# Sliding attention and a state-space convolution in one kernel: u kept in SBUF, v stored with its halo, the last matrix loaded by blocks, transfers split over two queues

## The chip, the cores and the metric

The kernel runs on one core of a Trainium2 chip. The core has five engines that run their own instruction streams: TensorE (PE; its weight loads are listed apart as PEld), VectorE (DVE), ScalarE (ACT), GpSimd (POOL) and SyncE (SP). SP, POOL and ACT also issue DMA transfers. The metric is the time of one launch in device microseconds; lower is better.

## The reference

Two independent computations over S = L = 2048 rows and D = 640 columns, put side by side in the output.

```python
# A: sliding, dilated attention. 32 heads of 20, window 8, dilation 2
q, k, v = x @ wqkv, split into heads
idx = pos[:, None] - (arange(8) * 2)[None, :]          # a row sees itself and 7 rows before it, 2 apart
logits = einsum("hsd,hswd->hsw", q, k[:, idx]) * 20 ** -0.5, -1e9 where idx < 0
a = einsum("hsw,hswd->hsd", softmax(logits), v[:, idx]).merge_heads() @ wo
# B: S4 convolution, 192 complex states for each of 640 channels
K[d, l] = real(sum_n C[d, n] * exp(dt[d] * A[d, n] * l) * dt[d] * B[d, n])
b = irfft(rfft(pad(u)) * rfft(pad(K)))[:, :2048] + u * Dskip
return concatenate([a, b], axis=-1)                    # 2048 x 1280
```

## The kernel before

**Part A (class `PartA`).** The rows go in four blocks of 512. `proj` multiplies x by wqkv for 128 columns at a time (L747), ScalarE copies the result to a staging tile `st` (L750), and SP stores it in DRAM: v to `vd` (L753), q and k to `qkd` (L755). Both have 14 columns of zeros in front (`halo`, L732 to L737, by POOL), so that a window that reaches back 14 rows always finds data. For block b, `fetch` (L767) reads five tiles `qk` of 128 channels back, each with 14 rows more, into three buffers; `fetch_v` (L780) reads v as 20 d's by 128 partitions (two halves of 256 rows, two parities of the window, 32 heads) into one tile of 8 d's and one of 12, with four transfers for each. `logits` multiplies q by shifted k on VectorE (`prod`, L793, ten for a block), sums over a head's channels on TensorE (L800) and makes the softmax; `av` multiplies attn by v (`p`, L842, ten for a block), sums on TensorE (L850); `out_proj` (L867 to L872) applies wo.

**Part B.** The channels go in five chunks c of 128, held as 4 groups of 32 (partitions: state or time index, depending on the stage). `Prep` makes tables of powers of exp(dt A); `Tables` builds for each chunk an x table (`Xtab`, with the gathered powers `Xg`, L539) and a y table (`Ytab`, L543; `ypos`, then `yneg`, L562 and L563, which multiplies by `mag`, L557). `kgen` (L596, L603) forms the convolution kernel from them on TensorE, ScalarE copies it (`Kd`, L617), SP moves Kd within SBUF (L584), and `spread` (L637, L642) lays it out as K. `f1` (L658) and `f2` (L678, `Sp` L683) transform K and the input u, whose chunk SP loads as tile `U` by four transfers of 64-byte runs (L1059). `swap` (L1073) brings the halves of a spectrum to the other partitions by two transfers; `product` (L688, L689) multiplies spectra on VectorE; `ia` (L703, L706) does the first inverse stage, whose Z is stored in DRAM for chunks 0 to 2 (L1084). At the end `inverse` adds, for each of 64 positions l, the identity times uD (u times Dskip, L1131) and the last inverse matrix HB times z (L1134), copies (L1137) and stores (L1139). HB is 128 x 128 for each l and each of real and imaginary part, zero outside four diagonal blocks of 32 x 32; eight transfers of 512 KB load it whole (L1103), eight of 320 KB load uD (L1108).

**The order.** Each function hands its work out as named pieces for the engines P, V, A, G (POOL and its queue) and S (SP's queue). `TRACE`, a recorded text, gives the order in which the pieces are created; `SEQ` gives each engine's own order, one engine after another; `SLOTS` says which buffer of a ring each piece takes. Every engine runs its list in that order. `attention_pool`, `fft_pool` and `inv_pool` free the SBUF of one phase for the next: HB and uD take the place of the tables (`tab`) and can be loaded only when the last `kgen` is done with them. In part A's names, `fetchv3.S` is a piece of `fetch_v(3)` on SP; in part B's, `yneg4` is `yneg` of chunk 4.

Of the kernel before, what the change touches and what calls it, by code (L numbers as in the profile page):

```python
# [18 lines left out]
CW = 192  # L19
# [6 lines left out]
S = 2048; D = 640; H = 32; DH = 20; W = 8; DIL = 2; HALO = 14; PB = 512; PH = 256  # L26
# [101 lines left out]
def att_consts_np():  # L128
    gs = np.zeros((128, 5, 32)); hs = np.zeros((128, 32)); sm = np.zeros((128, 128)); sw = np.zeros((128, 128)); mk = np.zeros((128, 4, 16))
    for p in range(128):  # L130
        for ct in range(5):
            gs[p, ct, (128 * ct + p) // DH] = 1.0
        hs[p, p % 32] = 1.0
        sm[p, 64 * (p // 64) + p % 32] = sm[p, 64 * (p // 64) + 32 + p % 32] = 1.0
        sw[p, p ^ 32] = -1.0
    for w in range(1, W):
        mk[32 * (w // 4):32 * (w // 4) + 32, 3 - w % 4, 0:DIL * w] = -1e9
    return dict(Gs=gs.reshape(128, 160), Hs=hs, Sm=sm, Sw=sw, Mk=mk.reshape(128, 64))
# [7 lines left out]
load.G weights.P mag0.A x1.S weights.A prep.V load.G weights.P weights.A gens0.V load.G prep.V weights.P weights.A gens0.V x1.S load.G prep.V
weights.V weights.A weights.P am0.A load.G prep.V am0.A weights.V am0.A wq.S load.G am0.A:2 x1.S set.G weights.V am0.A set.G am0.A:2 weights.V
am0.A:2 load.G x1.S weights.V am0.A prep.A weights.V load.G k0.P weights.S gens1.V load.G x2.S gens1.V load.G gens0.A gens1.A load.G gens1.V gens0.A
k0.P load.G gens1.A gens1.V load.G x3.S gens1.A weights.V gens1.A gens1.V k0.P genm0.V k0.A gens1.V x1.S gens1.A q0.P weights.V k0.A wv.S gens1.A
gens1.V q0.P weights.V x2.S q0.A gens1.V q0.P gens1.A x2.S weights.V k0.A q0.P weights.V gens1.A gens0.V x2.S weights.V q0.A q0.P gens0.V gens0.A  # L150
gens0.V gens0.A gens0.V q0.A weights.S k0.P gens0.V genm0.V gens0.A x2.S gens0.V gens0.A gens0.V gens0.A k0.P genm0.V gens0.A gens0.V gens0.A
gens0.V gens0.A x3.S genm0.V k0.A gens0.V:2 k0.A genm0.V gens0.V gens0.A xtab0.V k0.S v0.P gens0.A v0.P gens0.A gens0.V x3.S xtab0.V gens0.A xtab0.V
q0.A gens0.V:2 v0.P q0.A genm0.V gens0.V gens0.A xtab0.V q0.S gens0.A:2 gens0.V k1.P x3.S xtab0.V gens0.A gens0.V gens0.A gens0.V gens0.A xtab0.V
gens0.V gens0.A k1.P genm0.V gens0.A x3.S genm0.V xtab0.V k1.P xtab0.V genm0.V v0.A xtab0.V k1.P v0.A xtab0.V genm0.V v0.A xtab0.V k1.P v0.P genm0.V
xtab0.V am1.A xtab0.V v0.P v0.A genm1.V am1.A xtab0.V genm1.S v0.A k1.A v0.S q1.P:2 k1.A genm1.V k1.A q1.P k1.A gens1.V k1.A xtab0.V q1.P am1.A k1.S
xtab0.V genm1.S am1.A xtab0.V q1.P am1.A genm1.V v1.P am1.A xtab0.V genm1.S q1.A v1.P q1.A gens1.V q1.A v1.P xtab0.V q1.A genm1.V q1.A v1.P am1.A
q1.S xtab0.V genm1.S am1.A gens1.V k2.P xtab0.V am1.A k2.P xtab0.V am1.A v1.A gens1.V k2.P am1.A xtab0.V v1.A k2.P xtab0.V v1.A ypos0.V v1.A k2.P
ypos0.V k2.A ypos0.V:2 k2.A v1.P k2.A:2 ypos0.V k2.A ypos0.V v1.A k2.S q2.P yneg0.V q2.P v1.S q2.P gens1.A ypos0.V gens1.A q2.P gens1.A gens1.V q2.P
genm1.V q2.A:2 gens1.V v2.P genm1.S q2.A:2 ypos0.V q2.A v2.P gens1.A q2.S v2.P gens1.A gens1.V genm1.V gens1.A v2.P gens1.V v2.A genm1.S v2.A v2.P
genm1.V gens1.A k3.P gens1.V v2.A genm1.S ypos0.V v2.A:2 k3.P gens1.V gens1.A v2.S q3.P gens1.V gens1.A genm1.V gens1.A q3.P gens1.V genm1.S gens1.A  # L160
q3.P genm1.V gens1.A k3.A gens1.V genm1.S q3.P q3.A genm1.V q3.A q3.P gens1.V q3.A genm1.S q3.A ypos0.V k3.P q3.A gens1.A q3.S yneg0.V v3.P gens1.A
v3.P k3.A genm1.V k3.A v3.P yneg0.V genm1.S attpool fetch0.S v3.P gens1.A mag1.A fetch0.S v3.A:2 v3.P v3.A mag1.A:2 kgen03.P tab1.S mag1.A:2 wo.S
mag1.A:2 fetch0.S mag1.A k3.P mag1.A logits0.V fetchv0.S mag1.A:2 fetchv0.S mag1.A k3.P mag1.A fetchv0.S logits0.V mag1.A:3 k3.A kgen03.P logits0.V
fetch0.S k3.A v3.A k3.S logits0.P v3.A kgen02.P xtab1.V kgen03.A v3.S fftpool logits0.V fetchv0.S xtab1.V:2 logits0.V xtab1.V:5 logits0.P xtab1.V
kgen00.P xtab1.V:2 kgen00.P logits0.V xtab1.V:2 logits0.V u0.S fetch0.S xtab1.V u0.S logits0.P kgen00.A kgen01.P xtab1.V:2 u0.S xtab1.V kgen01.P
xtab1.V logits0.V u0.S xtab1.V:2 logits0.V logits0.P fetch1.S kgen01.A kgen02.P xtab1.V:2 kgen02.A ypos1.G taby1.S logits0.V ypos1.G taby1.S:2
xtab1.V logits0.P taby1.S xtab1.V taby1.S logits1.V T.S u0.P logits0.A u0.P kd0.S u0.A u0.P ypos1.V kd0.S u0.P u0.A logits1.V fetch1.S u0.P u0.A
u0.P fetchv0.S u0.P u0.A kd0.S ypos1.V u0.P ypos1.V u0.A logits0.V kd0.S u0.A u1.S ypos1.V u0.A:2 logits0.V ypos1.V logits0.P ypos1.V logits0.V
ypos1.V logits0.P spec.P logits0.A spec.P:2 spec.A fetchv0.S spec.A ypos1.V spec.P spec.A:2 spec.P spec.A tab2.S spec.A spec.P spec.A wo.S spec.A
logits1.V spread0.P fetch1.S spread0.P spec.A spread0.P spread0.A spread0.P fetch1.S spread0.A ypos1.V u1.S spread0.A ypos1.V spec.A:3 logits0.P  # L170
yneg1.V spread0.A spec.P:2 spec.A spread0.P spec.A spread0.P:2 spread0.A spread0.P yneg1.V spread0.P spec.A spread0.P spec.A spread0.P logits0.A
spread0.P mag2.A logits0.P mag2.A xtab2.V mag2.A u1.S logits0.A yneg1.V logits0.A mag2.A xtab2.V mag2.A kgen13.P xtab2.V mag2.A logits0.V mag2.A:3
wo.S mag2.A kgen13.P xtab2.V mag2.A swap0.S mag2.A:2 xtab2.V fetchv0.S xtab2.V mag2.A xtab2.V mag2.A u1.S spread0.A xtab2.V spread0.A xtab2.V
# [1016 lines left out]
```

## Time and profile before

| | before |
|---|---|
| time, median of 3 runs | 368.86 us (365.17 to 370.67) |
| the profiled execution: time, span | 369.83 us, 368.0 us |
| granted TensorE clock, mean | 0.903 |
| DVE busy | 305.1 us, 83% |
| PE busy | 292.8 us, 80% |
| ACT busy | 257.2 us, 70% |
| DMA | 119,210 packets, 65.49 MB, 178 GB/s over the span; 76,192 packets under 512 B |
| SP queue's share of 16 DMA engines | 71.6% |

The span is the time from the first to the last instruction of the profiled execution; the rest of its time, 1.8 us, lies outside. "Busy" counts an engine's instructions, not the issue of transfers. Ends of matmuls are modelled, so TensorE's busy time says less than the starts of its instructions do. In a line of groups the name before the arrow is what is written, the ones behind it are read; "idle before" is the time in which the engine stood idle just ahead of these instructions, with what ended the wait. "Issue" names idle time in which nothing that the profile shows was waited for.

### The profile page before, as it was taken

How to read it: one execution, taken by the hardware profiler on the slowest of the kernel's cores; microseconds unless marked ns; L12 is line 12 of the kernel's file. 1: busy time of each engine (PE TensorE's matmuls, PEld its weight loads, DVE VectorE, ACT ScalarE, POOL GpSimd, SP SyncE). 2: the span in 40 equal slices, each digit the busy share in tenths (PEclk: the TensorE clock that was granted, in tenths of full speed). 3: DMA queues.
4: the chain of work that ended last, by engine and by line, in shares of the span. 5: the costliest groups of instructions: out<-in, count | busy, mean ns of one | idle time of the engine just before them, and what ended most of it. 6: DMA issues, size and time to landing. Idle time of an engine off the chain costs nothing. (4 is left out here: it accounts for less than half of the span.)

```text
span 368.0 us, 13345 instructions
## 1 busy us (share of the span) xinstructions
PE 292.8 (80%) x5808; PEld 195.3 (53%) x5808; DVE 305.1 (83%) x397; ACT 257.2 (70%) x574; POOL 35.6 (10%) x72
## 2 busy tenths in 40 slices
PE   2959999999654486777989796888988748889984
PEld 1414444445431375555666564567855546557763
DVE  1896999795899988998999998799999935568940
ACT  2978899898600588357999645797779304779773
POOL 9740000000000000000000000000000000002750
PEclk9978999999665678899999899997999966999999
DMA  7999683697978987566976355860768756999885
GB/s 152 204 205 213 185 269 117 202 287 228 263 140 147 238 210 134 139 161 95 205 99 156 121 133 109 228 150 15 142 213 235 257 209 101 190 219 192 227 191 136
DMA packets 119210, 65.49 MB, mean 178 GB/s; under 512 B 76192, under 2 KB 115712, under 8 KB 118000
## 3 DMA queue, kind: packets, MB, share of 16 engines
q1 hardware_dynamic: 116320, 61.61, 71.6%
q0 software_dynamic: 1776, 2.79, 3.7%
q8 instruction: 45, 0.74, 0.9%
q10 hardware_dynamic: 1056, 0.25, 0.3%
q14 instruction: 13, 0.11, 0.1%
HBM read 35.25 MB, written 21.03 MB: 153 GB/s over the span
## 5 line engine op out<-in xcount | busy, mean ns | idle before, releaser
L747 PE MATMUL ps_p<-xT,w 128*128 128x512 bf16 x300 | 69.9, 397 | 4.1 <-DMA w<-in_A_wqkv_dram 4.1
L603 PE MATMUL ps_k<-Ytab,Xtab 64*20 64x33 bf16 (+1 forms) x2560 | 52.9, 247 | 11.7 <-issue 11.7
L842 DVE TENSOR_TENSOR p<-vb,attn 128x2048 bf16<-128x2048 bf16 x40 | 47.5, 1218 | 12.4 <-PE ps_o L850 10.3
L603 PEld LDWEIGHTS <-Xtab 64*20 64x20 bf16 (+1 forms) x2560 | 47.6, 123 | 17.0 <-issue 14.7
L793 DVE TENSOR_TENSOR prod<-qk 128x2048 bf16<-128x2048 bf16 x40 | 48.1, 1224 | 10.0 <-DMA qk<-qkd 7.5
L747 PEld LDWEIGHTS <-w 128*128 128x128 bf16 x300 | 30.2, 102 | 43.0 <-issue 6.2
L683 ACT CAST Sp<-ps_f 128x512 bf16<-128x512 f32 (+1 forms) x96 | 43.1, 613 | 7.0 <-PE ps_f L678 6.7
L662 ACT CAST A<-ps_f 128x512 bf16<-128x512 f32 x80 | 41.4, 619 | 7.1 <-PE ps_f L658 6.8
L617 ACT CAST Kd<-ps_k 128x264 bf16<-128x264 f32 x20 | 7.9, 394 | 47.0 <-PE ps_k L603 47.0
L750 ACT CAST st<-ps_p 128x512 bf16<-128x512 f32 x60 | 31.7, 609 | 7.1 <-DMA qkd<-st 3.1
L800 PE MATMUL ps_l<-prod,cGs 128*32 128x512 bf16 x160 | 21.5, 464 | 17.2 <-DVE prod L793 17.1
L678 PE MATMUL ps_f<-A,cT 64*128 64x128 bf16 (+1 forms) x768 | 27.7, 214 | 7.3 <-ACT Sp L683 3.5
L678 PEld LDWEIGHTS <-cT 64*128 64x128 bf16 x768 | 21.6, 98 | 16.4 <-issue 11.3
L706 ACT CAST Z<-ps_ia 128x512 bf16<-128x512 f32 x40 | 21.7, 632 | 5.6 <-PE ps_ia L703 5.6
L850 PE MATMUL ps_o<-p,cHs 64*32 64x256 bf16 x640 | 21.7, 288 | 4.1 <-DVE p L842 4.1
L867 PE MATMUL ps_op<-wo,oT 128*128 128x320 bf16 x160 | 24.4, 300 | 0.3 <-ACT oT L856 0.2
L547 POOL MEMSET Ytab<- 128x192 bf16 x5 | 1.3, 258 | 238.3 <-PE ps_k L603 134.4
L557 ACT ACTIVATE mag<-ta 128x192 bf16<-128x192 f32 x80 | 22.8, 404 | 0.0
L1139 POOL DMA_DIRECT2D out_dram<-ys x24 | 14.4, 608 | 76.8 <-ACT rc L826 70.2
L703 PE MATMUL ps_ia<-cE,Sp 128*128 128x128 bf16 x160 | 20.5, 224 | 0.7 <-DVE Sp L689 0.4
L510 DVE TENSOR_TENSOR krtmp<-Xtab,Xg 128x3072 bf16<-128x3072 bf16 (+1 forms) x15 | 20.3, 1356 | 0.1
L703 PE MATMUL ps_ia<-cE,UT 128*128 128x128 bf16 x160 | 20.4, 224 | 0.0
(113 smaller groups left out, 531.3 us busy)
## 6 DMA issues: line engine op xcount, KB each, us to landing
qk<-qkd SPq DMA_DIRECT2D x20, 263.0 KB
qkd<-st SPq DMA_DIRECT2D x8, 640.0 KB
UT<-Sp SPq DMA_DIRECT2D x10, 512.0 KB
Gdram<-cs SPq DMA_DIRECT2D x11, 384.0 KB
HB<-k_HB SPq DMA_DIRECT2D x8, 512.0 KB
vb<-vd SPq DMA_DIRECT2D x16, 196.5 KB
Xg<-Gdram SPq DMA_DIRECT2D x4, 768.0 KB
Zdram<-Z SPq DMA_DIRECT2D x3, 1024.0 KB
```

The source lines that it names most:

```text
L557: self.op("A", lambda b=b: self.nc.scalar.activation(out=self.mg[b // 8]()[:, b % 8], in_=ta()[:, s], func=ACT.Exp, scale=-16.0 * (b + 1)))
L603: MM(ps()[32 * g:32 * g + 20, i, :], lhsT=X()[k, :, p % 2, col], rhs=Y()[k, :, p % 2, col], start=False, stop=(p == order[3]), tile_positi ...
L662: op("A", lambda q=q, ps=ps: nc.scalar.copy(out=A1()[:].rearrange("p k r s t -> p (k r) s t")[:, :, sig, 8 * q:8 * q + 8], in_=ps()[:]))
L678: nc.tensor.matmul(ps[h]()[:, kk], lhsT=C["T"]()[hs, k, 64 * (1 - r):64 * (1 - r) + 128], rhs=A1()[hs, k, r, s0:s1, :].rearrange("p s t -> ...
L683: op("A", lambda q=q, h=h, ps=ps: nc.scalar.copy(out=Sp()[:, slots, h, :, 4 * q:4 * q + 4], in_=ps[h]()[:].rearrange("p k (s t) -> p s t k ...
L703: nc.tensor.matmul(ps()[:, i], lhsT=X()[:, h, 4 * t:4 * t + 4, :].rearrange("p g k -> p (g k)"), rhs=C["E"]()[:, n_, :], start=(i == 0 and ...
L706: op("A", lambda h=h, tq=tq, ps=ps: nc.scalar.copy(out=Z()[:, :, 16 * h + 4 * tq:16 * h + 4 * tq + 4], in_=ps()[:].rearrange("p t x -> p x ...
L747: nc.tensor.matmul(ps()[:], lhsT=self.w[which]()[:, kt, 128 * ct:128 * ct + 128], rhs=self.xT()[:, kt, 512 * sc:512 * sc + 512], start=(kt ...
L750: op("A", lambda ct=ct, ps=ps: nc.scalar.copy(out=st()[:, ct], in_=ps()[:]))
L793: op("V", lambda ct=ct, wg=wg, pr=pr: V.tensor_tensor(out=pr[wg]()[:], in0=self.qk[b][ct]()[:, 0, HALO:].unsqueeze(1).to_broadcast([128, 4 ...
L842: op("V", lambda t=t, qp=qp, v4=v4: V.tensor_tensor(out=v4(), in0=windows(self.v[b][t]()[:, 2 * qp:2 * qp + 2, 0:PH], 2, 4), in1=at()[:].u ...
L867: nc.tensor.matmul(ps()[:], lhsT=self.oT[b]()[:, t, 128 * s:128 * s + 128], rhs=self.wo_sb()[:, t, 320 * eh:320 * eh + 320], start=(t == 0 ...
```

## The change

1. u is loaded once, into uD in the pool of part A, early in the kernel, by eight transfers (four on SP, four on POOL). `f1` takes its weights from uD with a step of 160 elements; tile U and its 20 transfers are gone. The constant T moves to the same pool.
2. `vd` becomes eight halves of 640 channels by 272 columns with the 14 columns of halo inside; POOL copies the halo into the staging tiles, of which there are three instead of two. `fetch_v` reads groups of four d's into three buffers, half 0 by SP, half 1 by POOL, in runs of some 2 KB: 40 transfers on each queue instead of 32 on SP. The transfers of zeros (`halo`) are gone.
3. Block 3's q and k are used from the staging tiles and not stored; the blocks' order is 3, 0, 1, 2. The tiles `qk` have two buffers instead of three.
4. Of HB, POOL sets the whole tile to zero and four transfers load the diagonal blocks (1 MB in all instead of 4 MB, two on SP and two on POOL). The tile is laid out as 128 columns x 64 l x 2, so that L1134's 128 weight columns lie 128 elements apart.
5. The two transfers of `swap` go to SP and POOL. `mag` takes the buffer of Xg (for chunk 0 one in the preparation's pool); `spread`'s K takes a buffer of the ring of prod and p. The activation table is loaded at the start; wk (the first step of the angle) goes ahead; A_im is loaded before A_re.
6. TRACE, SEQ and SLOTS are written anew for all this.

```diff
 # PartA
-        self.qkd = dpool.tile([128, 5, 2, HALO + S], bf16, name="qkd")
-        self.vd = dpool.tile([H, DH, HALO + S], bf16, name="vd")
+        self.qkd = dpool.tile([128, 5, 2, S - PB], bf16, name="qkd")
+        self.vd = dpool.tile([S // PH, D, VW], bf16, name="vd")
...
 # proj
-        st = lazy(lambda: op.slot(self.pools["xw"], "st", 2, [128, 5, 512], bf16, "st"))
+        st = self.st[which, sc] = lazy(lambda: op.slot(self.pools["xw"], "st", 3, [128, 5, HALO + 512], bf16, "st"))
...
+            for half in range(2):
+                c0 = (512 + HALO - VW) * half
+                op("S", lambda half=half, c0=c0: nc.sync.dma_start(out=self.vd[2 * sc + half].rearrange("(c p) i -> p c i", p=128), in_=st()[:, :, c0:c0 + VW]))
...
 # fetch
+        if b == 3:
+            self.qk[b] = [(lambda ct=ct: self.st["q", 3]()[:, ct], lambda ct=ct: self.st["k", 3]()[:, ct]) for ct in range(5)]
+            return
-            t = lazy(lambda: self.op.slot(self.pools["att"], "qk", 3, [128, 2, HALO + PB], bf16, "qk"))
+            t = lazy(lambda: self.op.slot(self.pools["att"], "qk", 2, [128, 2, HALO + PB], bf16, "qk"))
...
 # fetch_v
-        for i, (d0, n) in enumerate(((0, 8), (8, 12))):
-            v = lazy(lambda i=i, n=n: self.pools["att"].tile([128, n, PH + 6], bf16, name="vb", tag=f"vb{i}", bufs=1))
+        for d0 in range(0, DH, 4):
+            v = lazy(lambda: self.op.slot(self.pools["att"], "vb", 3, [128, 4, VW], bf16, "vb"))
+            for half, (e, queue) in enumerate((("S", nc.sync), ("G", nc.gpsimd))):
+                src = self.vd[2 * b + half].rearrange("(h d) i -> h (d i)", d=DH)
+                for j in range(2):
+                    o = (VW - PH if half else HALO) - HALO + 8 * j
+                    r = 64 * half + 32 * j
+                    self.op(e, lambda v=v, r=r, queue=queue, src=src, o=o, d0=d0: queue.dma_start(out=v()[r:r + 32].rearrange("p d i -> p (d i)")[:, 0:4 * VW - o], in_=src[:, d0 * VW + o:(d0 + 4) * VW]))
...
 # Tables
-        self.mg = [lazy(lambda i=i: tp.tile([128, 8, CW], bf16, name="mag", tag=f"mag{i}", bufs=1)) for i in range(2)]
+        self.mg = lazy(lambda: (tp if c else pools["prep"]).tile([128, 16, CW], bf16, name="mag", tag="Xg" if c else "mag0", bufs=1))
...
 # u, spreading, swap
-        U = fft([128, 64, 32], bf16, name="U", tag="U")
-        for g in range(4):
-            op("S", lambda g=g: nc.sync.dma_start(out=U()[32 * g:32 * g + 32], in_=usrc[g, :, :, 32 * c:32 * c + 32]))
-        f1(tc, pools, op, C, [lambda: U()[:, :, 0:16], lambda: U()[:, :, 16:32]], "BU", A1s[c], c % 2)
+        f1(tc, pools, op, C, [lambda h=h: uD()[:, :, 32 * c + 16 * h:32 * c + 16 * h + 16] for h in range(2)], "BU", A1s[c], c % 2)
-        K = fft([128, 2, 64, 16], bf16, name="K", tag="K")
+        K = lazy(lambda: op.slot(pools["att"], "pr", 3, [128, 2, 64, 16], bf16, "K"))
+            e, queue = (("S", nc.sync), ("G", nc.gpsimd))[r]
...
 # the last matrix
-    HB = inv_([128, 64, 2, 128], bf16, name="HB")
-    uD = inv_([128, 64, 160], bf16, name="uD")
+    HB = inv_([128, 128, 64, 2], bf16, name="HB")
+    uD = lazy(lambda: pools["att"].tile([128, 64, 160], bf16, name="uD"))
-    def hb():
-        for q in range(8):
-            op("S", lambda q=q: nc.sync.dma_start(out=HB()[:, 8 * q:8 * q + 8].rearrange("p l r n -> p l (r n)"), in_=hsrc[:, 8 * q:8 * q + 8]))
+    def hb():
+        for g in range(4):
+            op("G", lambda g=g: nc.gpsimd.memset(HB()[:, 32 * g:32 * g + 32].rearrange("p n l r -> p (n l r)").bitcast(f32), 0.0))
+        for g in range(4):
+            r = slice(32 * g, 32 * g + 32)
+            e, queue = (("S", nc.sync), ("G", nc.gpsimd))[g // 2]
+            op(e, lambda g=g, r=r, queue=queue: queue.dma_start(out=HB()[r, r].rearrange("p n l r -> p (n l r)"), in_=hsrc[r]))
-                        nc.tensor.matmul(ps()[:, i], lhsT=HB()[:, l0 + o + i, r, :], rhs=z()[:, :, 2 * (o + i) + r, :], start=False, stop=(r == 1), skip_group_check=True)
+                        nc.tensor.matmul(ps()[:, i], lhsT=HB()[:, :, l0 + o + i, r], rhs=z()[:, :, 2 * (o + i) + r, :], start=False, stop=(r == 1), skip_group_check=True)
```

The order of VectorE's work near the end, from each SEQ (`:n` is the number of pieces in a row):

```
before: ... ypos4 av2 ypos4:2 yneg4:3 av2:5 prod3:4 av2 logits3:10 ud1 ud0 logits3:3 prod4:4 ud2 logits3 ud3 av3:10
after:  ... ypos4:2 logits2 ypos4:2 yneg4:2 logits2 yneg4 logits2:3 ud3 logits2 ud2 prod3 ud0 prod3:2 logits2 prod3 ud1 logits2:4 av2:4 prod4:3 av2 prod4 av2:5
```

More of the change, by code (lines that the diff above doesn't have):

```diff
@@ L146 @@
[L146 to L149, printed above, removed]
@@ new lines @@
+xtab4.V:2 prod2.V xtab4.V prod2.V xtab4.V:2 prod2.V xtab4.V:2 logits1.V xtab4.V:10 av1.V xtab4.V:2 av1.V xtab4.V:2 av1.V xtab4.V:2 av1.V:2 ypos4.V
+av1.V ypos4.V:2 av1.V:2 ypos4.V av1.V ypos4.V:2 av1.V ypos4.V:2 logits2.V ypos4.V:2 yneg4.V:2 logits2.V yneg4.V logits2.V:3 ud3.V logits2.V ud2.V
+prod3.V ud0.V prod3.V:2 logits2.V prod3.V ud1.V logits2.V:4 av2.V:4 prod4.V:3 av2.V prod4.V av2.V:5 ypos0.G params2.G:7 ypos0.G params2.G:5 set.G
+load.G:4 set.G load.G:9 v0.G:2 v1.G:2 k2.G v2.G k3.G v2.G v3.G fetch0.G:2 ud.G:4 fetchv3.G:6 ypos1.G:2 fetch0.G fetchv3.G:4 swap0.G fetch0.G:2
@@ new lines @@
+fetchv0.G:6 ypos2.G:2 swap1.G fetchv0.G:4 fetchv1.G:4 swap2.G fetchv1.G ypos3.G:2 fetchv1.G ypos4.G:2 swap3.G fetchv1.G:4 fetchv2.G:6 hb.G:4 swap4.G
+hb.G:2 fetchv2.G:4 last01.G:4 last03.G:4 last05.G:4 last13.G:4 last07.G:4 last11.G:4 params.S:7 params2.S wk.S params2.S x0.S x3.S params2.S x3.S
+x0.S params2.S x0.S:3 x3.S wq.S x1.S x3.S x1.S:3 weights.S x1.S x3.S wv.S x2.S q0.S x2.S:2 weights.S x2.S k0.S x2.S q1.S v0.S:2 genm1.S:2 v1.S k2.S
+v1.S genm1.S:2 k1.S genm1.S:3 q2.S v2.S:2 genm1.S:4 v3.S tab1.S fetchv3.S:6 fetch0.S v3.S ud.S:3 wo.S:4 ud.S kd0.S:4 taby1.S:4 T.S fetch0.S taby1.S
@@ new lines @@
+fetchv3.S:2 fetch0.S fetchv3.S:2 swap0.S tab2.S fetch0.S fetchv0.S:2 fetch0.S fetchv0.S:2 fetch1.S:2 fetchv0.S:2 out3.S taby2.S:5 kd1.S:4 out3.S:2
+fetch1.S swap1.S out3.S fetchv0.S:2 inv0.S fetch1.S fetchv0.S:2 tab3.S fetchv1.S:4 fetch1.S fetchv1.S:2 kd2.S:4 taby3.S out0.S taby3.S out0.S
+taby3.S inv1.S swap2.S taby3.S:2 fetch2.S:2 out0.S:2 tab4.S fetch2.S kd3.S:4 taby4.S:4 inv2.S fetchv1.S:2 taby4.S swap3.S fetchv1.S:2 fetchv2.S:2
+last01.S fetchv2.S:2 last01.S:2 last00.S:3 fetchv2.S:2 out1.S fetch2.S out1.S:3 fetch2.S kd4.S:4 hb.S:2 swap4.S fetchv2.S:4 last02.S:3 last03.S:3
@@ L556, in ymag @@
         for b in range(16):
-            self.op("A", lambda b=b: self.nc.scalar.activation(out=self.mg[b // 8]()[:, b % 8], in_=ta()[:, s], func=ACT.Exp, scale=-16.0 * (b + 1)))
+            self.op("A", lambda b=b: self.nc.scalar.activation(out=self.mg()[:, b], in_=ta()[:, s], func=ACT.Exp, scale=-16.0 * (b + 1)))
     def yneg(self):
@@ L730, in load_w @@
         self.op("S", lambda: self.nc.sync.dma_start(out=self.w[nm]()[:], in_=self.wqkv.rearrange("(kt k) c -> k kt c", k=128)[:, :, D * i:D * i + D]))
-    def halo(self):
-        nc = self.nc
-        z = lazy(lambda: self.pools["xw"].tile([128, 20 * HALO], bf16, name="zero"))
-        self.op("G", lambda: nc.gpsimd.memset(z()[:], 0.0))
-        self.op("G", lambda: nc.gpsimd.dma_start(out=self.qkd[:, :, :, 0:HALO], in_=z()[:, 0:10 * HALO].rearrange("p (c r i) -> p c r i", c=5, r=2)))
-        self.op("G", lambda: nc.gpsimd.dma_start(out=self.vd[:, :, 0:HALO], in_=z()[0:32, :].rearrange("p (d i) -> p d i", d=DH)))
     def proj(self, which, sc):
         nc, op = self.nc, self.op
-        st = lazy(lambda: op.slot(self.pools["xw"], "st", 2, [128, 5, 512], bf16, "st"))
+        st = self.st[which, sc] = lazy(lambda: op.slot(self.pools["xw"], "st", 3, [128, 5, HALO + 512], bf16, "st"))
         for ct in range(5):
@@ L749, in proj @@
             op("P", work)
-            op("A", lambda ct=ct, ps=ps: nc.scalar.copy(out=st()[:, ct], in_=ps()[:]))
-        s = slice(HALO + 512 * sc, HALO + 512 * sc + 512)
-        if which == "v":
-            op("S", lambda: nc.sync.dma_start(out=self.vd[:].rearrange("h d i -> (h d) i").rearrange("(c p) i -> p c i", p=128)[:, :, s], in_=st()[:]))
-        else:
-            op("S", lambda: nc.sync.dma_start(out=self.qkd[:, :, "qk".index(which), s], in_=st()[:]))
+            op("A", lambda ct=ct, ps=ps: nc.scalar.copy(out=st()[:, ct, HALO:], in_=ps()[:]))
+        if which == "v" or which == "k" and sc >= 2:
+            tail = self.halo.get(which)
+            if which == "v" and sc == 0:
+                op("G", lambda: nc.gpsimd.memset(st()[:, :, 0:HALO], 0.0))
+            elif which == "v" or sc == 3:
+                op("G", lambda: nc.gpsimd.tensor_copy(out=st()[:, :, 0:HALO], in_=tail()[:]))
+            if sc < 3:
+                self.halo[which] = lazy(lambda: self.pools["xw"].tile([128, 5, HALO], bf16, name="halo", tag="halo" + which, bufs=1))
+                op("G", lambda t=self.halo[which]: nc.gpsimd.tensor_copy(out=t()[:], in_=st()[:, :, 512:]))
+        if which == "v":
+            for half in range(2):
+                c0 = (512 + HALO - VW) * half
+                op("S", lambda half=half, c0=c0: nc.sync.dma_start(out=self.vd[2 * sc + half].rearrange("(c p) i -> p c i", p=128), in_=st()[:, :, c0:c0 + VW]))
+        elif sc < 3:
+            op("S", lambda: nc.sync.dma_start(out=self.qkd[:, :, "qk".index(which), 512 * sc:512 * sc + 512], in_=st()[:, :, HALO:]))
     def load_wo(self):
@@ L903 @@
     dst_b = out_b.rearrange("(l1 l0) (g ch) -> g l1 l0 ch", l0=64, g=4)
-    hsrc = bf_dram(nc, cn["HB"], "k_HB").rearrange("p (l x) -> p l x", l=64)
+    hbn = cn.pop("HB").reshape(4, 32, 64, 2, 4, 32)
+    hsrc = bf_dram(nc, np.stack([hbn[g, :, :, :, g].transpose(0, 3, 1, 2) for g in range(4)]).reshape(128, 64 * 2 * 32), "k_HB")
     pools = {}
@@ L1099 @@
         op.fill(f"out{b}", a.out_proj, b)
-    def hb():
-        for q in range(8):
-            op("S", lambda q=q: nc.sync.dma_start(out=HB()[:, 8 * q:8 * q + 8].rearrange("p l r n -> p l (r n)"), in_=hsrc[:, 8 * q:8 * q + 8]))
     def ud():
         for h in range(2):
-            for g in range(4):
-                op("S", lambda g=g, h=h: nc.sync.dma_start(out=uD()[32 * g:32 * g + 32, 32 * h:32 * h + 32], in_=usrc[g, :, 32 * h:32 * h + 32]))
+            for g in (0, 2, 1, 3):
+                e, queue = (("S", nc.sync), ("G", nc.gpsimd))[g // 2]
+                op(e, lambda g=g, h=h, queue=queue: queue.dma_start(out=uD()[32 * g:32 * g + 32, 32 * h:32 * h + 32], in_=usrc[g, :, 32 * h:32 * h + 32]))
     def udq(q):
@@ L1125, in inverse @@
         ysb = lambda: ys()[:, i, 0:nl * 32 * n].rearrange("p (l x) -> p l x", l=nl)
-        e, queue = (two[0], ("G", nc.gpsimd))[i % 2]
+        e, queue = (("S", nc.sync), ("G", nc.gpsimd))[i % 2]
         for o in range(0, nl, per):
```

345 lines of the change are left out of this document (178 added, 167 removed).

## The prediction, made before the changed kernel was run

> **What bounds the kernel now.** I read the engines' busy time first, then the slices, then what each engine waited for, then the last 80 us in the timeline.
>
> ```profile
> span 368.0 us, 13345 instructions
> ...
> PE 292.8 (80%) x5808; PEld 195.3 (53%) x5808; DVE 305.1 (83%) x397; ACT 257.2 (70%) x574; POOL 35.6 (10%) x72
> ...
> DVE  1896999795899988998999998799999935568940
> ...
> PEclk9978999999665678899999899997999966999999
> DMA  7999683697978987566976355860768756999885
> ```
>
> No engine is full. VectorE (DVE) is nearest: 305.1 us busy, 13.8 us after its last instruction (354.24), 49.2 us of gaps. Its dip in slices 32 to 35 (about 295 to 331 us) is the largest hole. So a change pays by closing DVE's gaps or by shortening what follows its last chain. DVE's waits over the span:
>
> ```profile
> DVE p L842 <- PE ps_o L850: 10.3, 2, 9.9
> DVE prod L793 <- DMA qk<-qkd: 7.5, 4, 4.1
> DVE dtf L427 <- ACT dtb L426: 5.8, 1, 5.8
> DVE m L813 <- PE ps_m L812: 3.7, 1, 3.7
> ```
>
> One wait of 9.9 us stands out (from 297.6 to 307.6), and only 7.5 us in all is a wait for the spilled q and k. The same place in the chain that ended last, and below it the longest line there of SP's queue waits:
>
> ```profile
> 291.08 1.40 PE ps_k L603 x61
> 292.48 3.71 issue
> 296.19 2.14 PE ps_k L603 x77
> 298.64 3.20 issue
> ...
> 304.35 0.94 issue
> ```
>
> ```profile
> SPq L1108 <- PE ps_k L603: 15.0, 1, 15.0
> ```
>
> TensorE (PE) stood 3.71, 3.20 and 0.94 us inside the last kernel generation (L603, chunk 4) with nothing that it waited for. In these microseconds the eight 512 KB loads of HB, issued from 286.2 to 291.5, were landing (381 GB/s from 292 to 297), and PE's instruction fetches ran beside them. I read the stalls as late instructions; that they sit together is shown, the cause is my reading. Meanwhile SP's queue held its next transfer (uD, L1108) 15.0 us for the same generation, and behind it Kd of chunk 4 (issued 308.5 to 312.3) and block 3's q and k.
>
> ```profile
> core 0: us, PE busy (x) PEld busy (x) DVE busy (x) ACT busy (x) POOL busy (x), PEclk, DMA share, GB/s
> 287.00:333.00 46.00, 34.09 (x926) 24.97 (x915) 27.56 (x26) 21.66 (x52) 0.00 (x0) 0.85 0.91 202
> 333.00:368.00 35.00, 27.98 (x550) 21.99 (x550) 20.37 (x17) 23.93 (x54) 14.42 (x24) 1.00 0.77 186
> ```
>
> These two rows are the case: a stretch of 46 us from the last Ytab (yneg4, 287.2) to the last spectrum (spec4, 333), with 12 us of PE idle, and a tail in which PE is busy 28.0 us of the 30 up to its end at 363.1.
>
> **The change, part by part.** The sum is made against the profiled execution: span 368.0, time 369.83, so 1.8 us outside. It is 1.0 above the median of 368.86.
>
> *Order.* DVE runs the same instructions, 302 us by the rows in both. But in the new order yneg4 comes after 272.7 us of DVE work instead of 263.6: **+9.1** up to that point, taken back only if the rest gets as much shorter.
>
> *Start.* The ACT table load of 1.28 us now runs ahead of the data, ident comes 0.9 us earlier, and flip(1) precedes flip(0), 1.4 us: wk about 3.2 us earlier. Against it DVE then waits for the first sine some 5 us and for B_re, now interleaved with x on SP, about 1. The first product of block 3 reads q and k from the staging tiles, so the 4.13 + 0.81 + 0.30 us of waits for fetch0 and Xg near 90 us go. −3.2 + 6.3 − 5.2: **−2**, between −5 and +3. The zero-halo transfers (L736, L737, 9.3 us to land, 4.6 us of wait on POOL) end no DVE wait; nothing for them.
>
> *Middle (90 to 290 us).* Nine products stand in a row while chunk 0's generation is on PE: +2.5 to +3.5. Fewer buffers: qk has two tiles instead of three; between release and reuse lie 3.9, 6.7, 8.6 and 8.6 us of DVE work at the tightest places, against 4.6 us from issue to landing (largest 8.8). vb has three of 4 d's instead of 8 and 12; four reuses have 4.4 to 6.9 us against 4.7. mag now lives in Xg's slot, so each Xg (5.2 us to land, 0.6 to issue) can start only after yneg's two L562 and has 5.0 to 5.8 us of cover: about +0.6 each, more if SP is held by an earlier wait. Behind the waiting Xg stand, on SP, q, k and v of block 0 (chunk 2), v of block 1 (chunk 3), and k, q of block 2 with Kd of chunk 3 and Ytab of chunk 4 (chunk 4): DVE's next products, PE's spread and DVE's next ypos. Together +1 to +6. Removed: half of the remaining waits for qk, Ytab and Xg (5.9 us), because 20 U loads (27 us of issue on SP) and five qk loads are gone: −1.5 to −3. **+3.5**, between −2 and +10. f1's lhsT now steps 160 elements instead of 32; its loads keep to pairs 88 ns apart under matmul pairs 107 apart, so I charge nothing; a step that doubled them would add 80 × 70 ns = 5.6 us, mostly in PE's idle time.
>
> *Queues.* POOL issues about 104 transfers instead of 41, at 0.58 to 0.65 us: some 40 us on a queue that stood nearly idle from 27 to 336 us. [...] Behind a POOL wait for a free vb tile stand swap's second half and the next halves of vb; behind HB's four memsets stand swap4 and the second pair of HB.
>
> *The stretch.* HB's load becomes four 256 KB transfers after generation, and uD is loaded 190 us earlier. PE's three stalls go: −7.9. Block 3's late q and k (2.1 us of DVE wait at 322.7) go with the held queue: −2.1. Kd4's four issues took 3.9 us among uD's and should take 1.8: −2. Eight pieces of the output projection (0.76 us each, L867) and four of av (0.62, L850) lie ahead of the stretch now, 8.6 us of PE work. The path there alternates between DVE, DMA and PE, so I take a third, −3. **−15**, between −19 and −6.
>
> *HB's zeros and its arrival.* Four POOL memsets of 128x2048 f32. Known rows are 128x280 bf16 at 0.351 us and 128x192 at 0.258, about 1.06 ns per element: 2.1 us each by elements, 4.3 by bytes, 8.5 to 17 in all. From the end of generation (about 310 by this sum) HB is whole at 310 + 8.5 to 17 + 6 us of landing (4.2 to 8 for similar sizes), 325 to 333, and needed at about 331. I charge nothing; +4 at the far end.
>
> *HB's stride.* L1134's 128 weight columns were contiguous and now lie 256 B apart.
>
> ```profile
> L658 PEld LDWEIGHTS <-U 128*64 128x64 bf16 x160 | 12.1, 198 | 5.2 <-issue 4.6
> L1134 PEld LDWEIGHTS <-HB 128*128 128x128 bf16 x256 | 11.7, 98 | 4.1 <-issue 1.2 <-DMA zb<-Zdram 0.9
> L658 PEld LDWEIGHTS <-K 128*128 128x128 bf16 x80 | 9.1, 145 | 2.8 <-issue 1.3 <-ACT K L642 1.1
> ```
>
> A strided load takes longer: 145 ns for K's 128 columns 32 B apart, 198 for U's 64 columns 64 B apart. What counts is how soon the next may follow. The closest starts in the trace are 38 to 56 ns for K and 88 to 90 for a pair of U's. HB's matmuls are 42 ns apart at N=96 (128 of them) and 29 at N=64 (128). With K's 45: 128 × (3 + 16) ns = +2.4. With U's 88: 128 × (46 + 59) ns = +13.4. K is a load of 128 columns like HB's, U is two of 64: I take K, **+2**, and keep 0 to +13.4.
>
> [...]
>
> *Sum.* 9.1 − 2 + 3.5 − 15 + 2 = −2.4: span 365.6, time 367.4 as profiled, about 366.5 on the scale of the median.
>
> **The rivals.**
> (a) *The order carries through* (faster). All 18.3 us of DVE's waits between 297 and 333 go (9.93, 2.47, 2.10, 3.75) and lighter DMA takes the middle to −2: 9.1 − 2 − 2 − 18.3 + 2 = −11.2. Time about 357.5. For it: the DVE row has 9 us less to do after yneg4. Against: PE has 62 us of work from 287 on and still does most of it.
> (b) *Weight loads bind the tail* (slower). If L1134's loads follow one another at U's 88 ns, the tail, where PE is full, grows by 11 us more: span 377, time about 378. It decides as soon as a load needs over some 60 ns. For it: U's step is nearer to HB's than K's. Against: U is not a 128-column load.
> (c) *The rings bind* (slower). Two qk tiles, three vb tiles and Xg behind mag make DVE wait 1.5 us at each of the four Xg and the eight tight qk and vb places, 18 instead of 3.5: time about 381. It decides once a landing takes over 7 us. For it: maxima of 8.8 (qk) and 8.7 (vb). Against: their medians, and 20 fewer loads.
> (d) *POOL's transfers starve beside DVE* (slower). If each POOL issue waited for DVE instructions, the two halves of vb at four tight places would come 2 × 1.2 us late each: +9.8, time about 376. The rows are against it: POOL issues of 576 to 651 ns, the same beside p at 1.22 us. [...]
>
> **How the numbers follow.** Forecast 0.38, (a) 0.32, (b) 0.15, (c) 0.11, (d) 0.04. Runs of before spread from 365.17 to 370.67, so 2% (7.4 us) is about what a measurement can tell from no change. Faster takes 0.29 of (a) and 0.05 of the forecast: 0.34. Slower takes 0.26 of (b), (c) and (d) and 0.03 of the forecast: 0.29. Within 2%: 0.37. The likeliest case alone reaches from 360 to 374; the range of all from 349 to 384.
>
> **What would show it.** Right: no stall of PE over 1 us in chunk 4's generation; yneg4 at 294 to 300; spec4 at most 36 us later; no DVE wait for qk near the first products; L1134's matmuls at most 50 ns apart. Wrong: DVE waits on qk, vb or Xg above 12 us in all (c); L1134's weight loads 80 ns or more apart (b); POOL issues above 1 us beside DVE (d); the first L1134 waiting for HB or its memset. A span under 358 with yneg4 before 290 would mean that the +9 and the +3.5 were not real.

## The result, and the profile after

| | before | after |
|---|---|---|
| time, median | 369.1 us (365.17 to 370.67, 4 runs) | 386.47 us (386.2 to 389.63, 4 runs) |
| ratio to before, 95% interval | | 1.053 [1.042, 1.063] |
| span of the profiled execution | 368.0 us | 384.6 us |
| DMA packets, MB | 119,210, 65.49 | 66,091, 57.33 |

Each ratio compares the executions of the faster of two states with executions of the kernel before taken beside them (medians of 371.2 to 372.2 us in the experiments), so it isn't the quotient of two medians of this text. The change made the kernel 5% slower, although it moves 8 MB less in 45% fewer packets. From the page after, the same rows as before:

```profile
span 384.6 us, 13447 instructions
...
PE 315.5 (82%) x5801; PEld 220.3 (57%) x5808; DVE 317.3 (83%) x397; ACT 275.1 (72%) x574; POOL 86.5 (22%) x134
...
DVE  3369999988998899998999994999999975799100
...
PEclk9999999999855879989999988598999988697598
DMA  6999458585999765203961157210983125555345
```

The hole in DVE's row near slice 33 is smaller, but the row now ends in 1, 0, 0 where it ended in 9, 4, 0: VectorE is done while the kernel goes on for three slices, 27.9 us instead of 13.8. Three engines have more busy time for the same instructions: PEld +25.0 us, DVE +12.2, ACT +17.9. The longest of VectorE's waits, and two ahead of products:

```profile
DVE wp L467 <- ACT Ytab L494: 8.2, 1, 8.2
DVE dtf L438 <- ACT dtb L437: 6.2, 1, 6.2
DVE attn L856 <- ACT rc L855: 5.3, 2, 4.6
...
DVE p L870 <- PE ps_o L878: 1.9, 2, 1.6
DVE prod L821 <- DMA qk<-qkd: 1.2, 1, 1.2
```

The wait of 9.9 us is gone, and of 7.5 us of waits for spilled q and k 1.2 are left. What is new lies in the rows of the two stretches (from yneg4's end to the last spectrum, and from there to the end), by the windows of each engine's busy time, two rows before and two after:

```profile
287.16:333.65 46.49, 34.58 (x925) 25.44 (x925) 27.64 (x27) 22.14 (x54) 0.00 (x0) 0.85 0.92 202
333.65:368.00 34.35, 27.33 (x541) 21.52 (x539) 20.14 (x17) 23.29 (x53) 14.42 (x24) 1.00 0.76 186
...
297.75:330.95 33.20, 27.09 (x791) 21.91 (x792) 23.48 (x22) 18.35 (x45) 10.51 (x11) 0.84 0.41 94
330.95:384.58 53.63, 48.28 (x523) 43.33 (x521) 25.75 (x10) 37.12 (x46) 17.70 (x24) 0.82 0.47 107
```

The first took 46.5 us before and takes 33.2; the second, the tail, took 34.35 and takes 53.6. In the second PE is busy for all but 5 us, with the same kinds of work. Groups of instructions, before and after, and the timeline of VectorE say why (the line of HB's loads before, 98 ns, is in the prediction):

```profile
L842 DVE TENSOR_TENSOR p<-vb,attn 128x2048 bf16<-128x2048 bf16 x40 | 47.5, 1218 | 12.4 <-PE ps_o L850 10.3 <-PE ps_l L800 2.1
...
L1137 ACT CAST ys<-ps_ib 128x384 bf16<-128x384 f32 x16 | 7.4, 485 | 2.9 <-PE ps_ib L1134 2.7
...
L870 DVE TENSOR_TENSOR p<-vb,attn 128x2048 bf16<-128x2048 bf16 x40 | 59.8, 1586 | 2.9 <-PE ps_o L878 1.9 <-DMA vb<-vd 0.8
...
L1169 PEld LDWEIGHTS <-HB 128*128 128x128 bf16 x256 | 34.5, 267 | 1.6 <-issue 0.8
...
L1172 ACT CAST ys<-ps_ib 128x384 bf16<-128x384 f32 x16 | 13.8, 903 | 4.4 <-PE ps_ib L1169 4.2
```

```profile
326.85 1.22 DVE L870 TENSOR_TENSOR p<-vb,attn 128x2048 bf16<-128x2048 bf16 x1
330.70 3.27 DVE L704 TENSOR_TENSOR UT<-Sp,UT 128x2048 bf16<-128x2048 bf16 x1 [2.64 <-ACT Sp L699]
334.01 1.95 DVE L705 TENSOR_TENSOR Sp<-Sp 128x2048 bf16<-128x2048 bf16 x1
335.88 1.20 DVE L704 TENSOR_TENSOR UT<-Sp,UT 128x2048 bf16<-128x2048 bf16 x1
337.00 2.98 DVE L870 TENSOR_TENSOR p<-vb,attn 128x2048 bf16<-128x2048 bf16 x1
339.89 1.23 DVE L705 TENSOR_TENSOR Sp<-Sp 128x2048 bf16<-128x2048 bf16 x1
341.01 15.72 DVE L870 TENSOR_TENSOR p<-vb,attn 128x2048 bf16<-128x2048 bf16 x5
```

A weight load of HB takes 267 ns instead of 98, and from the starts in the trace HB's matmuls follow one another 127 ns apart (N=96) and 122 (N=64) instead of 42 and 29: 128 x (85 + 93) ns = 22.8 us, of a tail that grew by 19.3 (PE's idle time in the tail fell from 7.02 to 5.35 us; the rest of the difference is not accounted for). The first 34 of VectorE's products p take 1.22 us each, and five of the last six take 2.2 to 6.5 us: while HB's loads run (from 330.1 us), instructions of other engines, which read other tiles, get slower too. The one of the six that no load of HB overlaps, at 343.7 us, takes 1.25 us. ScalarE's copies of 128x384 take 903 ns on average instead of 485.

The granted clock in the tail fell too, from 1.00 to 0.82. That isn't what spaces the loads: in the stretches at half the granted clock their median spacing is 120 ns, at full clock 128. What the lower clock costs TensorE's other work in the tail wasn't measured apart.

### The profile page after: what moved, and what is told of

It reads as the page before. It is cut to its first block, busy times and chain, and to the rows that moved or that the text cites. A ratio compares the mean times of both kernels' runs of the same rounds, so it can differ in the third digit from the quotient of the medians.

```text
span 384.6 us, 13447 instructions
## 1 busy us (share of the span) xinstructions
PE 315.5 (82%) x5801; PEld 220.3 (57%) x5808; DVE 317.3 (83%) x397; ACT 275.1 (72%) x574; POOL 86.5 (22%) x134
## 2 busy tenths in 40 slices
DMA packets 66091, 57.33 MB, mean 149 GB/s; under 512 B 32064, under 2 KB 61312, under 8 KB 64752
## 5 line engine op out<-in xcount | busy, mean ns | idle before, releaser
L757 PE MATMUL ps_p<-xT,w 128*128 128x512 bf16 x293 | 65.8, 383 | 0.4
L870 DVE TENSOR_TENSOR p<-vb,attn 128x2048 bf16<-128x2048 bf16 x40 | 59.8, 1586 | 2.9 <-PE ps_o L878 1.9
L619 PE MATMUL ps_k<-Ytab,Xtab 128*20 128x33 bf16 (+1 forms) x2560 | 52.5, 247 | 4.9 <-issue 3.9
L619 PEld LDWEIGHTS <-Xtab 128*20 128x20 bf16 (+1 forms) x2560 | 47.0, 123 | 10.7 <-issue 7.8
L821 DVE TENSOR_TENSOR prod<-qk 128x2048 bf16<-128x2048 bf16 x30 | 36.4, 1227 | 1.2 <-DMA qk<-qkd 1.2
L808 POOL DMA_DIRECT2D vb<-vd x40 | 19.9, 503 | 75.2 <-DVE p L870 58.8
L1169 PEld LDWEIGHTS <-HB 128*128 128x128 bf16 x256 | 34.5, 267 | 1.6 <-issue 0.8
L1172 ACT CAST ys<-ps_ib 128x384 bf16<-128x384 f32 (+1 forms) x24 | 22.9, 1007 | 9.0 <-PE ps_ib L1169 8.8
L1174 POOL DMA_DIRECT2D out_dram<-ys x24 | 17.7, 759 | 33.3 <-ACT ys L1172 26.9
L769 POOL COPY halo<-st 128x70 bf16<-128x70 bf16 x4 | 14.4, 3610 | 45.0 <-ACT st L760 45.0
L828 PE MATMUL ps_l<-prod,cGs 128*32 128x512 bf16 x160 | 18.3, 421 | 4.9 <-DVE prod L821 4.7
```

Source lines behind the costliest of these rows:

```text
L619: MM(ps()[32 * g:32 * g + 20, i, :], lhsT=X()[k, :, p % 2, col], rhs=Y()[k, :, p % 2, col], start=False, stop=(p == order[3]), tile_positi ...
L757: nc.tensor.matmul(ps()[:], lhsT=self.w[which]()[:, kt, 128 * ct:128 * ct + 128], rhs=self.xT()[:, kt, 512 * sc:512 * sc + 512], start=(kt ...
L821: op("V", lambda ct=ct, wg=wg, pr=pr: V.tensor_tensor(out=pr[wg]()[:], in0=self.qk[b][ct][0]()[:, HALO:].unsqueeze(1).to_broadcast([128, 4 ...
L870: op("V", lambda t=t, qp=qp, v4=v4: V.tensor_tensor(out=v4(), in0=windows(self.v[b][t]()[:, 2 * qp:2 * qp + 2, 0:PH], 2, 4), in1=at()[:].u ...
L1169: nc.tensor.matmul(ps()[:, i], lhsT=HB()[:, :, l0 + o + i, r], rhs=z()[:, :, 2 * (o + i) + r, :], start=False, stop=(r == 1), skip_group_c ...
```

## The experiments

The theory after this comparison: the step of L1169's weight columns is the loss, and the rest of the change does about what was forecast. The rival: the tail is long because HB comes late (it was whole at 329.9 us, and its first matmul ran at 330.1), or because of POOL's queue.

**1. Columns side by side again.**

```diff
-    HB = inv_([128, 128, 64, 2], bf16, name="HB")
+    HB = inv_([128, 128, 128], bf16, name="HB")       # [matrix 2 l + r, column]
-... lhsT=HB()[:, :, l0 + o + i, r]
+... lhsT=HB()[:, 2 * (l0 + o + i) + r]
```

> The changed kernel with HB's 128 weight columns side by side again (step 1), still only the diagonal blocks, now in runs of 64 bytes (16,384 of them instead of 128 of 8 KB). Theory (the step of the weight loads is the loss): matmuls of the last inverse back at 42 and 29 ns apart instead of 127, the tail after the last spectrum back from 53.6 to about 35 us, VectorE's products and ScalarE's copies in the tail back at 1.22 and 0.53 us; time 364 to 370, unless the small runs land late (then the first of these matmuls waits for HB by several us). Rival (late HB behind the memsets, or the outputs on POOL's queue): the tail stays above 48 us and the time above 380.

Measured: 378.76 us, 1.017 [1.009, 1.024] of before, above the 364 to 370 expected for a load in time. Spacing 43 and 29 ns, p at 1.22 us: the step is most of the loss. But 64-byte runs landed late (one HB transfer 13.3 us after its issue, a half of UT beside them 15.4), and HB's first matmul came at 337.3, 5.6 us behind the last spectrum. VectorE's waits show the second victim, the swap:

```profile
DVE UT L704 <- DMA UT<-Sp: 7.6, 1, 7.6
```

**2. A step of 16 elements, and 3. the kernel before with a step of 128.**

```diff
 # 2: after
-    HB = inv_([128, 128, 64, 2], bf16, name="HB")
+    HB = inv_([128, 8, 128, 16], bf16, name="HB")
+... lhsT=HB()[:, (2 * (l0 + o + i) + r) // 16, :, (2 * (l0 + o + i) + r) % 16]
 # 3: before
-    HB = inv_([128, 64, 2, 128], bf16, name="HB")
+    HB = inv_([128, 128, 128], bf16, name="HB")       # [column, 2 l + r]
+... lhsT=HB()[:, :, 2 * (l0 + o + i) + r]
```

> The changed kernel with HB laid out in 8 groups of 16 matrices, so that the 128 weight columns lie 16 elements (32 bytes) apart, as K's do; the blocks land in runs of 1 KB. If the cost of a strided load depends on the step as the reading of K's closest starts (38 to 56 ns) says: matmuls 42 to 56 ns apart, tail 36 to 40 us, time 365 to 371. If any step other than 1 costs the same as 128: spacing above 100 ns, tail above 48 us, time above 380.

Measured: 380.04 us, 1.023 [1.017, 1.029]. Spacing 62 to 64 ns, between the two theories' values; VectorE's p at 1.22 us and ScalarE's copies at 0.48, their old durations. Here a memset of HB waited for a transfer of another block (3.9 us, twice), and HB was whole only at 339.9, so that the time says little of the step. Run 7 mends that.

> The kernel before with only the layout of HB changed: 128 weight columns 128 elements apart, loaded whole in the same eight transfers. Theory: the last inverse's matmuls go from 42 and 29 to about 127 ns apart, the tail grows by 15 to 19 us, time 384 to 388, and VectorE's and ScalarE's instructions beside them get longer than 1.22 and 0.53 us. Rival (the loss needs the other parts of the change): time within 4 us of 369.

Measured: 396.54 us, 1.063 [1.054, 1.072]: 25 us slower by the layout alone, more than the 15 to 19 expected. Spacing 127 ns, and p 1627 ns on average (1586 in the changed kernel):

```profile
L842 DVE TENSOR_TENSOR p<-vb,attn 128x2048 bf16<-128x2048 bf16 x40 | 62.8, 1627 | 14.3 <-PE ps_o L850 11.5 <-PE ps_l L800 2.6
...
L1134 PEld LDWEIGHTS <-HB 128*128 128x128 bf16 x256 | 34.5, 267 | 1.6 <-issue 0.8
```

So the loss needs nothing else of the change: neither late HB nor POOL's queue, for here SP loads HB whole, as before.

**4. The kernel before with HB's load behind the last kernel generation** (`hb.S:8` moved behind `kd4` and two tiles of `fetch3` on SP).

> The kernel before with HB's eight transfers issued behind the last kernel generation (after two tiles of q and k of block 3) instead of ahead of it. If the transfers' burst caused the three stalls of TensorE there (3.71, 3.20 and 0.94 us): none above 1 us is left, the last Kd copy comes 6 to 8 us earlier, and the time falls by 3 to 8 us. Rival (the stalls have another cause): they stay, time within 2 us of 369.

Measured: 381.63 us, 1.030 [1.022, 1.039], so the time went the other way. The stalls did fall, from 7.9 us (first line, before) to 2.6:

```profile
PE ps_k L603 <- issue: 7.9, 3, 3.7
...
PE ps_k L603 <- issue: 2.6, 2, 1.4
```

and the last Kd copy came at 303.5 instead of 307.0. But the 4 MB then stood ahead of uD, vb and swap4: UT landed at 340.7 instead of 331.5 and the last spectrum came at 342.9, 9.2 us later. Most of the stalls went with HB's burst, by a mechanism that isn't shown, and in its new place the burst cost more.

**5, 6. Other steps, and a step that is no power of two.** Two kernels with two tiles of HB each:

```diff
+    HBs = [inv_([128, 64 // s, 128, s], bf16, name=f"HB{j}") for j, s in enumerate((2, 64))]     # and (4, 32)
```

> The changed kernel with HB in two tiles: weight columns 2 elements apart for the first 32 positions l, 64 apart for the last 32. If the cost grows with the step (42 ns side by side, 62 at 16, 127 at 128): first half 42 to 50 ns at N=96, second half 85 to 115, and VectorE's and ScalarE's instructions get longer only beside the second half. If what counts is only whether columns are side by side: both halves 60 ns or more.

> The same with steps of 4 (first 32 positions) and 32 (last 32). If the cost grows with the step: first half 42 to 55 ns, second half 65 to 95. VectorE's products of 1.22 us beside the second half tell from which step on other engines are slowed: if they stay at 1.22 here, only steps above 32 elements (64 bytes) do it.

The changed kernel with four elements of padding:

```diff
-    HB = inv_([128, 128, 64, 2], bf16, name="HB")
+    HB = inv_([128, 128, 132], bf16, name="HB")
```

> The changed kernel with each weight column 132 elements (264 bytes) apart instead of 128 (256): only the padding differs. If the slow loads and the slowed neighbours come from addresses a power of two apart that fall on the same part of the memory: spacing back to 62 ns or near it and VectorE at 1.22 us, time about 370. If any far step is as slow: about 127 ns, VectorE up to 6 us, time about 386.

Each of the three ran once. Measured, median spacing of HB's weight loads by their starts, with the other runs:

| step, elements (bytes) | N=96, ns | N=64, ns | one load, ns | p of VectorE beside it |
|---|---|---|---|---|
| 1 (2), before | 42 | 29 | 98 | 1.22 us |
| 2 (4) | 43 | 29 | 98 | 1.22 us |
| 4 (8) | 43 | 33 | 117 | 1.22 us |
| 16 (32) | 63 to 64 | 62 | 164 | 1.22 us |
| 32 (64) | 62 | 60 | 163 | 1.22 us |
| 64 (128) | 91 | 89 | 218 | 1.22 us |
| 128 (256) | 127 | 122 | 272 | 2.2 to 6.5 us, five of six |
| 132 (264) | 67 to 74 | 65 | 172 | 1.22 us |

At half the granted clock N=96 takes 80 ns at the steps of 1, 2, 16 and 132 alike. The cost isn't simply one of the distance: 264 bytes (65 to 74 ns) are nearly as fast as 32 or 64 (60 to 64), 256 bytes take twice as long (122 to 127), and only they slow the other engines. The group of p in the padded kernel, against 1586 ns at a step of 128:

```profile
L870 DVE TENSOR_TENSOR p<-vb,attn 128x2048 bf16<-128x2048 bf16 x40 | 48.1, 1220 | 7.7 <-PE ps_o L878 6.5 <-DMA vb<-vd 1.1
...
L1169 PEld LDWEIGHTS <-HB 128*128 128x128 bf16 x256 | 20.8, 171 | 3.2 <-issue 2.1
```

The padded run's 65 to 74 ns are the outcome that was set down for addresses a power of two apart falling on the same part of the memory; no run shows such parts, and that 32 and 64 bytes cost the same (62 to 64 and 60 to 62 ns) does not follow from it. The padded kernel took 380.33 us, where 370 was expected. The spacing came back to about 65 ns and the tail to 40.6 us, but the last spectrum came at 338.0, 7 us later than in the changed kernel, though VectorE's work up to yneg4 is the same in both (see the account of the prediction). The kernels of two tiles took 379.98 and 378.56 us with a last spectrum at 337.4 and 336.8; none of the three times says what a step is worth.

**7. Step 16 with HB's load in time.** The four memsets are made ahead of all transfers of HB, and POOL's two transfers ahead of swap4 (in the changed kernel they waited for it until 320.7 us).

```diff
-hb.G:4 swap4.G hb.G:2
+hb.G:6 swap4.G
```

> The changed kernel with step 16, and the four memsets and then POOL's two transfers of HB ahead of the swap of chunk 4 on its queue. HB is then whole by about 325 instead of 330 to 340. If the step and the late HB are all that the change lost: tail about 40 us from a last spectrum at 331, time 370 to 374. If something else holds the tail: above 378.

Measured: 374.11 us, 1.006 [1.001, 1.011]; from the last spectrum at 335.8 PE needed 33.8 us to its end, against 29.4 before.

**8, 9. Steps 4 and 2 with HB's load in time.**

> The changed kernel with step 4 (runs of 256 bytes in the load) and the memsets and POOL's two transfers of HB ahead of the swap. Matmuls 42 and 34 to 36 ns apart (seen at this step), VectorE at 1.22 us in the tail, HB whole before the last spectrum. If the step was the whole loss and the rest of the change is worth what the stretch showed: tail 35 to 37 us, time 1 to 2% under the kernel before. If the rest is worth nothing: within 1% of before.

> The same with step 2 (runs of 128 bytes, 8,192 of them). Matmuls 42 and 29 apart, 1 us less in the tail than at step 4 if the load lands in time; if small runs land late, the first matmul of the last inverse waits for HB by 2 to 6 us and the time is that much above step 4's.

Measured: 370.49 us, 0.994 [0.991, 0.998], for step 4, and 370.87 us, 0.992 [0.986, 0.997], for step 2. Both beat the kernel before, by less than 1%. That isn't the 1 to 2% expected for step 4, but the other case that was set down there, within 1%: the rest of the change worth nothing, or nearly so. With step 4 the tail is 36.2 us (332.67 to 368.84), the spacing 43 and 33 ns:

```profile
332.67:368.84 36.17, 28.45 (x520) 22.39 (x517) 11.62 (x10) 21.70 (x47) 14.37 (x24) 0.92 0.77 173
```

So PE's work in the tail is back near the 27.3 us of before, but the tail is 1.8 us longer than before's, and the last spectrum came only 1.0 us earlier (332.67 against 333.65). HB now stands ahead of the swap: the halves of UT landed 11.6 us after their issue instead of 5.1 and 6.7 in the changed kernel, and VectorE waited 4.2 us for them. The late landing feared for step 2's small runs did not decide: HB was whole when its first matmul was due, and its loads kept to 43 and 29 ns.

**10. The kernel before with blocks of HB only**, step 4, everything else as it was.

```diff
-hb.S:8 ud.S:2 kd4.S:2
+hb.S:4 ud.S:2 kd4.S:2          # and hb.G:4, the memsets, on POOL
```

> The kernel before with only HB's load changed: POOL sets HB to zero and four transfers of 256 KB load the diagonal blocks, step 4, in the place of the eight of 512 KB. If the size of the burst made TensorE stand still in the last kernel generation: its stalls fall from 7.9 us to under 3 (2.6 with the load moved behind), the last Kd copy comes 3 to 6 us earlier, nothing is pushed back behind it, and the time falls by 2 to 6 us. Rival (the time is set elsewhere): within 1 us.

Measured: 367.85 us, 0.987 [0.980, 0.994], in four executions: this one part alone makes the kernel faster, by 1.3%, and is the fastest version by its ratio (its interval overlaps those of steps 2 and 4). The time fell as expected; the mechanism is only half shown: TensorE's stalls fell to 4.8 us, not to under 3, and the last Kd copy came 1.7 us earlier, not 3 to 6. The four transfers now start behind the memsets, at 296 us, and the slow stretch moved with them (first row before, then this run):

```profile
292.00:297.00 5.00, 1.29 (x70) 1.02 (x62) 4.93 (x5) 0.00 (x0) 0.00 (x0) 0.96 1.02 381
...
292.00:297.00 5.00, 4.14 (x214) 3.65 (x206) 4.96 (x5) 0.77 (x2) 3.92 (x3) 1.00 0.02 5
297.00:302.00 5.00, 2.51 (x128) 2.23 (x128) 1.91 (x2) 0.38 (x1) 0.00 (x0) 0.69 1.12 159
```

From 292 to 297, with 5 GB/s moving, PE is busy for 4.14 us; in the kernel before, with 381 GB/s, it was 1.29. From 297 to 302 the transfers land, and it is 2.51.

## Why the prediction was wrong, point by point

*The forecast* was 366.5 us and no change within 2%, with a range up to 384; measured 386.47. Its steps against the trace of the changed kernel:

- *Order, start, middle.* yneg4 ended at 297.75, 10.6 us later than before; the three terms gave 9.1 − 2 + 3.5 = 10.6. That they agree is partly luck. The parts were less exact than their sum: VectorE's busy time up to that point is 10.8 us longer (268.1 against 257.3), not 9.1, and the first product came 3.4 us earlier (88.91 against 92.30), not 2, though the wait for the first sine was there (8.2 us). And 10.6 is the low end: up to yneg4 runs 1, 2, 7 and 8 have the same VectorE instructions as the changed kernel, in the same order, and yneg4 ended at 298.9 to 302.4 in them. This spread from execution to execution is larger than the whole forecast of −2.4; its cause is open. VectorE waited 1.2 us for qk, 0.8 for vb and 3.2 for Ytab.
- *The stretch.* −13.3 us; −15 was forecast. PE's stalls in chunk 4's generation went from 7.9 to 1.3 us, and run 4, where they fell to 2.6, showed that HB's load had a part in them. That late instructions were the cause is not shown: in the trace of before, packets of an instruction queue start at 293.9 and 299.4 us, within two of the three stalls, but nothing there ties the stalls to them.
- *HB's zeros.* 1.80 us for each memset, 7.0 in all; the estimate by elements was 2.1 each, that by bytes was wrong. HB was whole at 329.9, inside 325 to 333: POOL's pair stood 3.1 us behind swap4's wait and took 7.5 and 8.2 us to land.
- *f1's step of 160 elements.* Nothing was charged, rightly: a load of uD takes 196 ns, one of U took 198.
- *HB's stride.* This is the step that failed: +2 was charged, from K's closest starts, with U's 88 ns as the far end (+13.4). It was 127 and 122 ns, and the tail grew by 19.3 us. −2.4 with 19.3 in the place of 2 is +14.9; the span grew by 16.6.

Two things were wrong in that step. K's closest starts (38 to 56 ns) are those of the first two loads of a series, when the second runs ahead; further ones were hidden under matmuls 109 ns apart, so K never showed its own rate. At K's step HB's loads repeat every 62 ns, which alone would have been 128 x (21 + 33) ns = +6.9. And the row nearest by shape was taken to stand for a step eight times as large, although the far end should have been open: no row of before has 128 columns at 256 bytes. The longest bound in hand, K's hidden 109 ns, would have given 128 x (67 + 80) = +18.8, and was left out of the range.

*The rivals.* (b), the weight loads that bind the tail, is what happened, at 127 ns instead of 88: it had 0.15. It lacked the second half, that other engines get slower (VectorE's products of 1.22 us at up to 6.5). (a) is half right: VectorE's waits of 18.3 us between the last Ytab and the last spectrum became 9.6 (2.4, 4.6 and 2.6), so 8.7 of the 18.3 went; the last spectrum came 2.7 us earlier. (c), the rings, is refuted by VectorE's waits of 2 us on qk and vb. (d), POOL starving beside VectorE, is refuted too for transfers:

```profile
L808 POOL DMA_DIRECT2D vb<-vd x40 | 19.9, 503 | 75.2 <-DVE p L870 58.8 <-DMA vd<-st 13.0 <-DMA zb<-Zdram 3.3
L769 POOL COPY halo<-st 128x70 bf16<-128x70 bf16 x4 | 14.4, 3610 | 45.0 <-ACT st L760 45.0
```

A POOL issue of vb takes 503 ns, less than the 576 to 651 of most of POOL's issues before. POOL's own copies are another matter: the same copy of 70 elements, with VectorE at work beside it throughout, takes 1.0 to 6.6 us; why was not tested. ScalarE waited 1.2 us for them.

*What the change is worth without that step.* At step 2 or 4 and HB in time, 0.992 and 0.994 of before; the forecast, 366.5 of 368.86, was 0.994. That match bears out no single term: in the trace of step 4 they come to +13.1 us up to yneg4, −14.1 in the stretch and +1.8 in the tail, +0.8 in all against the trace of before. Run 10, with HB's blocks alone, reached 0.987, so no gain of the other five parts together is shown.

## What to carry to other kernels

Before a layout is changed so that a transfer gets long runs, look at who reads the tile: in these runs the distance between weight columns went with how soon the loads followed one another (29 to 43 ns at 1 and 2 elements, 122 to 127 at 128), and 256 bytes was the worst of the distances tried, for the reader and for its neighbours (products of 1.22 us at up to 6.5). A compromise cost nearly nothing here: with 2 to 4 elements between columns the loads kept to 43 ns (N=96) and 29 to 33 (N=64), in runs of 128 to 256 bytes. And take a rate only from a row in which the operation itself is the limit: K's loads, at 145 ns each, started 109 ns apart beside matmuls at the same spacing, and HB's loads at the same step followed 62 ns apart.

## What the runs showed of the hardware that was not expected

- HB's 128-column weight loads at N=64 repeated every 29 ns at steps of 1 and 2 elements and every 33 at 4; at both N every 60 to 64 at 16 and 32, 89 to 91 at 64, 122 to 127 at 128 and 65 to 74 at 132. At N=96 steps of 1, 2 and 4 gave 42 to 43 ns alike, so there the step did not set the pace. At 128 the spacing is nearly the same at half and at full clock, 120 and 128 ns.
- Beside loads at a step of 256 bytes, VectorE's 1.22 us multiplication took up to 6.5 us, ScalarE's 0.48 us copy up to 1.38, and POOL's issue of 0.58 us up to 1.35. Beside all other steps the multiplication kept its 1.22 us, and in the runs of steps 1, 2, 4, 16 and 132 the copy took 480 to 490 ns and the issue of an output 606 ns on average.
- 256 KB in runs of 64 bytes landed 7.2 to 13.3 us after issue (run 1). In runs of 8 KB the same four transfers took 3.3 and 3.9 us on SP, 7.5 and 8.2 on POOL behind the swap.
